# Filler matmuls around the first transposes, one product moved in each expert's last weight chunk, and one set of weight sums issued later: a routed mixture of experts behind linear attention

## The chip, the cores and the metric

The kernel runs on one core of one Trainium2 chip. The metric is the device time of one execution in microseconds (us). Three executions of the kernel before took 555.15 us (median), from 554.48 to 555.25. A core has a matrix engine (PE, with its weight loads shown apart as PEld), a vector engine (DVE), a scalar engine (ACT), a general engine (POOL) and a queue that only issues DMAs (SP). Each engine works through its own list in order; semaphores tie the lists together. PE writes to PSUM only, and ACT and DVE read it from there.

## The reference

```python
kv  = einsum('bhsd,bhse->bhde', k, v)          # 8 batches, 8 heads, s = 576, d = 64, no softmax
out = einsum('bhsd,bhde->bhse', q, kv)
x   = out / sqrt(mean(out*out, -1) + 1e-6) * g_norm      # 4608 tokens of 512 values
e_idx = argmax(x @ w_gate)                     # one of 8 experts for each token
gate  = softmax(x @ w_gate)[e_idx];  eom = sigmoid(x @ w_output_gate)
for e in range(8):                             # each token goes through its expert alone
    h = relu(x[e_idx == e] @ w1[e])            # 512 -> 1024
    y[e_idx == e] = gate * eom[:, e] * (h @ w2[e])       # 1024 -> 512
```

All inputs and outputs are float32.

## The kernel before

**First part: attention and routing.** For each batch PE builds `kv` (`kv_step`), then the 36 row tiles of `out`, 128 tokens each (`out_tile`). ACT squares them, DVE sums the squares (`sums`), and `route` works out experts, weights and row numbers for three groups of tiles (16, 10 and 10) in steps. Rows go to a buffer in device memory (`xs`), from which POOL gathers each expert's tokens by index. `p1_main` sets the order of this part by hand. After the last row tile it works through the string `TAIL`, letter by letter in `act` (L1010): `Q` evacuates the rows left, `W` issues weight loads, a digit takes the next step of that group's routing, `C` calls `constant` and `L` takes the next step of `lead_run`. `constant(ps, n)` (L685) issues n bfloat16 matmuls of ones by ones, 256 columns wide here, whose results nobody reads. `C` issues eight of them into a PSUM tile of the pool `ps_b` (three buffers, tag `big`).

`lead_run` starts the fullest expert before the routing of the last group is known. Its first two steps (`stage`, L280) each take one gathered tile of 128 tokens: DVE scales it by its norms, PE transposes it in four matmuls (L296), ACT copies it out (L299). Its next eight (`lead1`, L317) are the first layer for one eighth of the hidden values each, four full float32 matmuls (L325). Between those steps the string puts routing of group 2, whose rank matmuls (L888 to L895) stand behind the second `lead1`.

**Second part: experts.** `RUNS` has nine runs. Run 0 is the lead, run 1 the rest of the lead expert, runs 2 to 8 are the other seven experts with room for 656, 632, 608, 592, 572, 560 and 544 tokens. Each float32 operand is split into a rounded high part and a residual low part, and each product is three matmuls (high by high, high by low, low by high). From run 2 on the first layer is done by a scheme of seven products instead of eight per pair of blocks: `seven(i)` is a generator that goes through four weight chunks (c = 0 to 3), and `begin(i, n)` takes its next n steps. For one chunk, `a` and `d` are two PSUM tiles (`hpsa`, `hpsd`):

- 11 into `a`, copied by ACT to `sn[0]`; S3 into `d`; 12 into a third tile; S2 added into `a`, copied to `sn[1]`;
- S1 added into `a`, copied by ACT to `sn[2]` (L545); DVE adds `d` and `sn[2]` (L546); then `split_h` makes the hidden values: ACT applies relu (L499), DVE subtracts for the residual (L502);
- `late3`: S4 added into `a`, which must wait for the copy L545; then `split_h` straight from PSUM;
- `late4`: 22 with T4 added into `d`, which must wait for DVE's read of `d` (L546); DVE adds `d` and `sn[1]` (L513) and `split_h` follows on twice the width.

The `late` steps of a chunk are issued within the next chunk: between S2 and S1 of chunk c stand `late3(c - 1)` and `late4(c - 1)`.

The second layer is `mm2(i, k, events)`: tile k of run i, eight f-steps of three matmuls 128x512 (L591), with `events` called after each f-step. The first tile of a run carries the last two steps of `seven`, `late3(3)` behind f = 0 and `late4(3)` behind f = 1. What comes after it for the next run is put in the same way (`put`, L1271): `x_stage(i + 1, k)` behind f = 2 of tile k (PE transposes two gathered tiles, L445, ACT and DVE make the operands, L454 to L464), `x_sums` behind f = 7 (L471, L472), `sums_of(i + 1, c)` behind f = 1 of tile c - 1, `scale_rows` behind f = 3 of the first tile, `w_split` later. `sums_of` is `w_sums` (L382): four POOL instructions (L387 to L390) that form sums and differences of weight blocks. `scale_rows` is one POOL instruction per gathered tile (L270), which is told to start only behind a certain DVE instruction (`latest`): the two behind f = 3 start behind L458 and L461 of the `x_stage` at f = 2.

In this text the seam of a run is the stretch from its last S1 to the end of its first second-layer tile.

## Time and profile before

| | |
|---|---|
| median of three executions | 555.15 us (554.48 to 555.25) |
| the profiled execution | 558.12 us |
| span of its instructions | 556.3 us |
| PE, PEld busy | 536.3 us (96%), 459.4 us (83%) |
| DVE, ACT, POOL busy | 388.7 us (70%), 296.1 us (53%), 264.6 us (48%) |
| mean granted clock of TensorE | 0.992 |

Busy shares are means over stages with different limits. A PE that is 96% busy leaves 20 us of idle time, and a busy PE can be at half of its clock; both are found only by looking at the stretch in question. In the rows of a timeline a bracket at the end gives the idle time of the engine just before the instruction and what ended it.

### The profile page before, as it was taken

The numbers are of one execution on the slowest core, as the hardware profiler recorded it, in microseconds if no ns is written. First come the engines' busy times: TensorE is split into PE (matmuls) and PEld (weight loads), VectorE is DVE, ScalarE is ACT, GpSimd is POOL, SyncE is SP. The second block draws the span as 40 slices with busy tenths as digits, with TensorE's granted clock in tenths as the row PEclk, the third lists the DMA queues.
The fourth block names the chain that finished last, engine by engine and source line by source line (L and its number), as shares of the span: only waits on it lengthen the run. The fifth ranks groups of instructions, "written<-read, shape, count | busy, mean of one in ns | idle before, by whom it ended". The sixth has DMA issues, their size and how long they took to land.

```text
span 556.3 us, 10940 instructions
## 1 busy us (share of the span) xinstructions
PE 536.3 (96%) x4076; PEld 459.4 (83%) x4076; DVE 388.7 (70%) x828; ACT 296.1 (53%) x604; POOL 264.6 (48%) x283
## 2 busy tenths in 40 slices
PE   9999986999999999999999999999999999999995
PEld 7798885856988978898789878987798789789974
DVE  2135998666699789567976896687578977996600
ACT  1577773143467637364646474646473856475410
POOL 3001224054897288208941792289228933981021
PEclk9999999799999999999999999999999999999999
DMA  8999999653406340616052605251534055214000
GB/s 301 418 417 415 416 395 413 254 185 121 131 1 210 111 140 38 209 41 206 20 189 80 199 38 190 92 163 39 189 93 156 38 193 157 78 64 167 1 37 31
DMA packets 28423, 92.27 MB, mean 166 GB/s; under 512 B 3825, under 2 KB 3825, under 8 KB 28368
## 3 DMA queue, kind: packets, MB, share of 16 engines
q1 hardware_dynamic: 21936, 71.63, 35.5%
q0 software_dynamic: 6432, 19.92, 10.7%
q8 instruction: 33, 0.54, 0.4%
q14 instruction: 22, 0.18, 0.1%
HBM read 72.34 MB, written 19.70 MB: 165 GB/s over the span
## 4 chain that ended last, share of the span: by engine, by line
PE 66%; DVE 14%; DMA 6%; POOL 5%; issue 4%; ACT 3%; SPq 1%; POOLq 0%; DVEq 0%; ACTq 0%
PE yps L591 27%; PE hpsa L479 13%; PE hpsd L479 6%; PE hps L479 4%; PE hps L346 3%; PE yps L585 3%; PE hps L325 3%; DVE hT L502 3%; PE ops L781 2%; DVE ss L807 2%; DMA ld<-qT 2%; DMA xg<-xs,gidx 2%; DMA ld<-kvm 2%; PE kvp L706 2%; POOL xg L270 2%
## 5 line engine op out<-in xcount | busy, mean ns | idle before, releaser
L591 PE MATMUL yps<-whi,hT 128*128 128x512 f32 (+3 forms) x560 | 184.9, 396 | 0.4 <-DVE hT L502 0.4
L591 PEld LDWEIGHTS yps<-whi,hT 128*128 128x128 f32 (+3 forms) x560 | 103.8, 186 | 24.2 <-DVE hT L502 1.3
L591 PE MATMUL yps<-wlo,hT 128*128 128x512 f32 (+3 forms) x280 | 110.0, 393 | 0.0
L605 POOL DMA_INDIRECT out<-y,oidx x42 | 52.0, 1237 | 111.7 <-ACT y L604 76.0
L252 POOL DMA_INDIRECT xg<-xs,gidx x42 | 45.0, 1071 | 96.7 <-ACT hT L499 28.2
L502 DVE SCALAR_TENSOR_TENSOR hT<-ct,hT 128x256 fp32r<-128x256 f32 (+6 forms) x88 | 52.2, 623 | 22.7 <-ACT hT L499 21.8
L591 PEld LDWEIGHTS yps<-wlo,hT 128*128 128x128 f32 (+3 forms) x280 | 52.1, 186 | 9.9
L499 ACT ACTIVATE hT<-ct 128x328 fp32r<-128x328 f32 (+13 forms) x56 | 34.4, 615 | 43.0 <-DVE ct L513 43.0
L270 POOL TENSOR_TENSOR xg<-xg 128x512 f32<-128x512 f32 (+8 forms) x40 | 46.5, 1175 | 10.1 <-DVE ct L534 9.5
L479 PE MATMUL hpsd<-xT,wh 128*128 128x328 f32 (+6 forms) x224 | 48.0, 302 | 1.6 <-DVE ct L546 1.6
L479 PE MATMUL hpsa<-xb,wh 128*128 128x328 f32 (+6 forms) x224 | 48.2, 303 | 1.1 <-ACT sn L545 0.6
L479 PE MATMUL hpsa<-xT,wh 128*128 128x328 f32 (+6 forms) x224 | 47.4, 299 | 0.0
L229 DVE TENSOR_TENSOR wlo<-wraw,whi 128x1024 fp32r<-128x1024 f32 x32 | 40.3, 1260 | 6.5 <-ACT whi L226 6.3
L807 DVE TENSOR_REDUCE ss<-sq 128x8 f32<-128x512 f32 x36 | 23.8, 681 | 30.1 <-ACT sq L797 30.1
L404 DVE SCALAR_TENSOR_TENSOR wl<-wraw,gcol,wh 128x512 fp32r<-128x512 f32 (+1 forms) x56 | 42.6, 800 | 0.1
L781 PE MATMUL ops<-aug,ld 64*128 64x80 f32 (+1 forms) x640 | 39.4, 271 | 1.9 <-ACT gp L798 1.5
L479 PEld LDWEIGHTS hpsa<-xb,wh 128*128 128x128 f32 x224 | 36.6, 188 | 4.9 <-ACT sn L545 3.6
L479 PEld LDWEIGHTS hpsd<-xT,wh 128*128 128x128 f32 x224 | 36.6, 188 | 4.7 <-DVE ct L546 3.9
L604 ACT ACTIVATE y<-yps,tl 128x512 f32<-128x512 f32 (+3 forms) x37 | 25.5, 689 | 28.0 <-PE yps L591 18.7
L404 DVE SCALAR_TENSOR_TENSOR wl<-ws,gcol,wh 128x1024 fp32r<-128x1024 f32 x28 | 40.0, 1429 | 0.0
L781 PEld LDWEIGHTS ops<-aug,ld 64*128 64x128 f32 (+1 forms) x640 | 33.9, 176 | 5.3 <-ACT gp L798 1.7
L479 PEld LDWEIGHTS hpsa<-xT,wh 128*128 128x128 f32 x224 | 37.0, 188 | 1.5
(231 smaller groups left out, 1150.4 us busy)
## 6 DMA issues: line engine op xcount, KB each, us to landing
wraw<-w SPq DMA_DIRECT2D x64, 512.0 KB
ld<-kvm SPq DMA_DIRECT2D x32, 512.0 KB
ld<-qT SPq DMA_DIRECT2D x18, 512.0 KB
xs<-xrow SPq DMA_DIRECT2D x9, 528.0 KB
xs<-xrow SPq DMA_DIRECT2D x2, 1320.0 KB
xs<-xrow SPq DMA_DIRECT2D x1, 2112.0 KB
ld<-rem SPq DMA_DIRECT2D x4, 512.0 KB
xg<-xs,gidx POOLq DMA_INDIRECT x42, 5.0
```

The lines of the kernel that those rows point to most:

```text
L229: eng.tensor_tensor(out=lo, in0=r, in1=hi.bitcast(F32), op=ALU.subtract)
L252: gathered = nc.gpsimd.indirect_dma_start(out=x[:M, :], out_offset=None, in_=rows, in_offset=bass.IndirectOffsetOnAxis(ap=gidx[:M, p, t:t ...
L270: return eng.tensor_tensor(out=v, in0=v, in1=f, op=ALU.mult)
L404: nc.vector.scalar_tensor_tensor(out=lo, in0=x, scalar=gcol[:, 0:1], in1=hi.bitcast(F32), op0=ALU.mult, op1=ALU.subtract)
L479: nc.tensor.matmul(ps, W[a][d], X[b][d], start=start and k == 0, stop=k == 5, skip_group_check=not start)
L499: S.activation(hh, x, AF.Relu)
L502: V.scalar_tensor_tensor(out=v(o, j1 - j0), in0=x[..., j0:j1], scalar=0.0, in1=hh[..., j0:j1].bitcast(F32), op0=ALU.max, op1=ALU.subtract)
L591: nc.tensor.matmul(ps[:M], a, b, start=(f == 0 and j == 0), stop=(f == 7 and j == 2))
L604: nc.scalar.activation(y[:M], ps[:M], AF.Copy, scale=tl[:M, 0:1])
L605: i_ = nc.gpsimd.indirect_dma_start(out=out, out_offset=bass.IndirectOffsetOnAxis(ap=oidx[:M, p, t:t + 1], axis=0), in_=y[:M], in_offset=N ...
L781: nc.tensor.matmul(v[r0:r0 + m, u, p, :], qt[g // 2][r, p, q0:q0 + m], augs[b % 3][r, p, :], start=True, stop=True)
L807: nc.vector.tensor_reduce(out=o, in_=sq, axis=AX.X, op=ALU.add)
```

## The change

Three edits. In `TAIL` two more `C` (sixteen matmuls) stand ahead of the lead's first transposes, and a new letter `c` behind each of the two transposes issues six of the same matmuls into a part of `kvp` that is no longer read. In `seven`, for c = 3 alone, `late4(2)` moves from ahead of S1 to behind it. The number of steps of the generator stays 28. The sums of weight chunk 1 for the next expert are issued behind f = 4 of the first tile instead of f = 1, in runs 2 to 7, and so behind `x_stage` (f = 2) and the two `scale_rows` (f = 3).

```diff
-TAIL = "QW112CCCCCCCLL2L2L22L2L1L2L1K2LL"
+TAIL = "QW112CCCCCCCCCLcLc2L2L22L2L1L2L1K2LL"
@@ seven
             if c:
                 late3(c - 1)
                 yield
+            if c in (1, 2):
                 late4(c - 1)
                 yield
             product(a, w_of(c, "S1"), x_of(i, "T1"), False)
...
             split_h(c, 0, 0, ct[:, 2 * n:3 * n])
             yield
+        late4(2)
+        yield
         late3(3)
         yield
         late4(3)
@@ act
+        elif step == "c":
+            constant(kvp[:, 256:512], 6)
@@ body
                 for c in range(1, 4):
-                    put(order[c - 1], 1, sums_of, p + 1, c)
+                    put(order[c - 1], 4 if c == 1 and i > 1 else 1, sums_of, p + 1, c)
```

Of the kernel before, what the change touches and what calls it, by code (L numbers as in the profile page):

```python
# [71 lines left out]
PLACES = ['VP', 'VP', 'V']  # L72

HOOKS = {35: "G"}
TAIL = "QW112CCCCCCCLL2L2L22L2L1L2L1K2LL"

COLD = (24, (8, 8, 10, 5), 5, 4, 12, 8)

# [57 lines left out]
def body(ctx: ExitStack, tc: tile.TileContext, kvm, rem, qT, wg, gn, w1, w2, kc, xs, tab, out):  # L136
# [31 lines left out]
    kvp, mrp = (ps_y.tile([P, 512], F32, name=n, tag=t) for n, t in (("kvp", "y0"), ("mrp", "y1")))  # L168
# [4 lines left out]
    def take(shape, dt, name):  # L173

        i = (rfree if name == "xrow" else free).pop(0)
        t = mem.tile(shape, dt, name=name, tag=f"slot{i}")
        held[id(t)] = (i, t)
        return t

    def give(t):  # L180
        i, t = held.pop(id(t))
        (rfree if loads and i >= SLOTS - ROWS else free).append(i)
# [12 lines left out]
    def wload(p, which, c, eng=None):  # L195
        r = take([P, 1024], F32, "wraw")
        eng = eng or nc.sync
        src = (w1 if which == 1 else w2)[ds(expert(p, eng), 1), c]
        d = eng.dma_start(out=r, in_=src.rearrange("o p x -> p (o x)"))
        raw[(p, which, c)] = r  # L200
        return d
# [106 lines left out]
    def half(i):  # L308

        n = RUNS[i][2] % P  # L310
        return n if n <= P // 2 else 0

    def place(i):

        return -(-half(i) // 32) * 32
# [94 lines left out]
    def w_drop(c):  # L410
        for w in wop.pop(c):
            give(w)

    def w_of(c, name):
        h0, l0, h1, l1 = wop[c]
        k = ("11", "12", "22").index(name) if name[0] != "S" else int(name[1]) - 1
        a, b = (h1, l1) if name[0] == "S" else (h0, l0)
        return [[x[:, 2 * k + d] for d in range(2)] for x in (a, b)]

    def x_of(i, name):  # L420
        bh, bl, th, tl = xop[i]
        k = ("11", "21", "22").index(name) if name[0] != "T" else int(name[1]) - 1
        a, b = (th, tl) if name[0] == "T" else (bh, bl)
        return [[x[:, 2 * k + d] for d in range(2)] for x in (a, b)]
# [50 lines left out]
    def product(ps, W, X, start):  # L475
        k = 0
        for d in range(2):
            for a, b in ((0, 0), (0, 1), (1, 0)):
                nc.tensor.matmul(ps, W[a][d], X[b][d], start=start and k == 0, stop=k == 5,  # L479
                                 skip_group_check=not start)  # L480
                k += 1

    def seven(i):

        nonlocal ny
        p, _, C = RUNS[i]
        n = C // 2
        st = {}
        S, V = nc.scalar, nc.vector

        T, U = half(i), place(i)
        C0 = C - T

        def split_h(c, f, a, x):

            h = hT[i][:, 2 * c + f]
            v = lambda o, k: h[:, o:o + 2 * k].rearrange("q (k a) -> q a k", a=2)[:, a]
            hh = v(0, n)
            S.activation(hh, x, AF.Relu)  # L499
            cut = C0 // 2  # L500
            for o, j0, j1 in ((C0 + 2 * U, 0, cut), (C0 + U, cut, n)) if T else ((C, 0, n),):
                V.scalar_tensor_tensor(out=v(o, j1 - j0), in0=x[..., j0:j1], scalar=0.0,  # L502
                                       in1=hh[..., j0:j1].bitcast(F32), op0=ALU.max, op1=ALU.subtract)

        def late3(c):
            a, d, sn, ct = st[c]
            product(a, w_of(c, "S4"), x_of(i, "22"), False)
            split_h(c, 0, 1, a)

        def late4(c):  # L510
            a, d, sn, ct = st.pop(c)
            product(d, w_of(c, "22"), x_of(i, "T4"), False)
            latest[0] = V.tensor_tensor(out=ct[:, 0:n], in0=d, in1=sn[:, 1], op=ALU.add)  # L513
            split_h(c, 1, slice(0, 2), ct[:, 0:2 * n].rearrange("q (a k) -> q a k", a=2))
            give(st.pop(("sn", c)))
            give(st.pop(("ct", c)))
            w_drop(c)

        for c in range(4):
            a, d = (pools["two"].tile([P, 512], F32, name=f"hps{x}")[:, 0:n] for x in "ad")  # L520
            st["sn", c] = take([P, 1024], F32, "sn")
            st["ct", c] = take([P, 1024], F32, "ct")
            sn = st["sn", c][:, 0:3 * n].rearrange("q (s n) -> q s n", s=3)
            ct = st["ct", c][:, 0:3 * n]
            st[c] = (a, d, sn, ct)
            product(a, w_of(c, "11"), x_of(i, "11"), True)
            S.copy(sn[:, 0], a)
            yield
            product(d, w_of(c, "S3"), x_of(i, "T3"), True)
            yield  # L530
            b = ps_y.tile([P, DM], F32, name="hps2", tag=f"y{ny % 2}")[:, 0:n]
            ny += 1
            product(b, w_of(c, "12"), x_of(i, "21"), True)
            latest[0] = V.tensor_tensor(out=ct[:, 2 * n:3 * n], in0=b, in1=sn[:, 0], op=ALU.add)  # L534
            yield
            product(a, w_of(c, "S2"), x_of(i, "T2"), False)
            S.copy(sn[:, 1], a)
            yield
            if c:
                late3(c - 1)  # L540
                yield
                late4(c - 1)
                yield
            product(a, w_of(c, "S1"), x_of(i, "T1"), False)
            S.copy(sn[:, 2], a)  # L545
            latest[0] = V.tensor_tensor(out=ct[:, n:2 * n], in0=d, in1=sn[:, 2], op=ALU.add)  # L546
            if c == 0:
                hT[i] = hp.tile([P, 8, 2 * C0 + 2 * U], F32R, name="hT")
                if T < U:
                    for o in (C0 + T, C0 + U + T):  # L550
                        V.memset(hT[i].bitcast(F32)[:, :, o:o + U - T], 0.0)
            split_h(c, 0, 0, ct[:, 2 * n:3 * n])
            yield
        late3(3)
        yield
        late4(3)
        xop.pop(i)
        yield
# [126 lines left out]
    def constant(ps, n, start=True):  # L685

        for _ in range(n):
            k = ps.shape[1] // P
            nc.tensor.matmul(ps, ones, ones.unsqueeze(1).to_broadcast([P, k, P]), start=start, stop=start)
# [291 lines left out]
    def advance(gi):  # L981
        if next(routing[gi], 2) == 2:
            del routing[gi]
# [26 lines left out]
    def act(step):  # L1010
        if step.isdigit():
            advance(int(step))
        elif step == "W":
            for c in range(4):
                wload(0, 2, c)
        elif step == "K":
            ranks()
        elif step == "Q":
            while outs:
                out_rows()  # L1020
            while squares:
                sums()
        elif step == "G":
            free.extend(rfree)
            rfree.clear()
            gather(0)
        elif step == "C":
            constant(ps_b.tile([P, 2, 512], F32, name="cps", tag="big")[:, 0, 0:256], COLD[5])
        else:
            next(lead, None)  # L1030

    def p1_main():
# [16 lines left out]
        while done_tiles < NT:  # L1049
            run_out(NT)  # L1050
        for step in TAIL:
            act(step)
# [148 lines left out]
    with tc.manual_schedule(engines=MAN):  # L1201
# [12 lines left out]
        for i in range(len(RUNS)):  # L1214
            p = RUNS[i][0]
# [55 lines left out]
            def put(k, f, e, *a):  # L1271
                at.setdefault(k, {}).setdefault(f, []).append(lambda: e(*a))

            order = list(range(T))
# [11 lines left out]
                        put(order[0], 1, wload, p + 1, 1, c)  # L1286
            if change:
                for c in range(1, 4):
                    put(order[c - 1], 1, sums_of, p + 1, c)
                if i == 1:  # L1290
                    places = [(1, 0, 4), (2, 3, 0), (3, 3, 4)]
                else:
                    places = [(0, 1, 4), (1, 2, 4), (2, 3, 1), (3, 3, 5)]
                for c, k, f in places:
                    put(order[k], f, w_split, p + 1, c)
                for k in range(3):
                    put(order[k], 2, x_stage, i + 1, k)
                    put(order[k], 7, x_sums, i + 1, k)
                for j in range(2):
                    k = 3 + j + (i == 1)  # L1300
                    put(order[0], 3, scale_rows, i + 1, k, k + 1, j)
                put(end, 0, wload, p + 1, 2, 0)
                for c in range(3):
                    put(end, 2 * c + 1, drop, 2, c)
                    put(end, 2 * c + 1, wload, p + 1, 2, c + 1)
                for f, n in ((1, 1), (3, 2), (5, 1), (8, 1)):
                    put(end, f, begin, i + 1, n)
# [116 lines left out]
```

## Rows read from the trace of the kernel before

**Rows 1.** Page part 2: granted PE clock in 40 equal slices of the span.
```profile
PEclk9999999799999999999999999999999999999999
```
**Rows 2.** Timeline of PE, 84 to 112 us: start, duration, instruction, idle before.
```profile
88.09 4.53 PE L689 MATMUL cps<-ones 128*128 128x256 bf16 x40 [0.17 <-PE cps L689]
94.65 0.63 PE L296 MATMUL tps<-ident,xg 128*128 128x128 f32 x4 [2.03 <-DVE tl L292]
96.00 0.63 PE L296 MATMUL tps<-ident,xg 128*128 128x128 f32 x4 [0.73 <-DVE tl L292]
97.41 6.75 PE L325 MATMUL hps<-xT,wraw 128*128 128x256 f32 x16 [0.78 <-ACT xT L299]
...
104.39 7.14 PE L325 MATMUL hps<-xT,wraw 128*128 128x256 f32 x32
```
**Rows 3.** Window of 1 us: PE, PEld, DVE, ACT, POOL busy, clock, DMA, GB/s.
```profile
97.00:98.00 1.00, 0.59 (x2) 0.50 (x3) 1.00 (x2) 0.36 (x1) 0.00 (x0) 0.50 1.04 399
```
**Rows 4.** Timeline of DVE at the routing of group 2.
```profile
104.59 0.24 DVE L911 TENSOR_TENSOR rw<-mrp,ohb 128x80 f32<-128x80 f32 x1 [3.46 <-PE mrp L895]
```
**Rows 5.** Timeline of POOL: the first gather for run 1.
```profile
117.08 1.04 POOL L252 DMA_INDIRECT xg<-xs,gidx  x1 [20.71 <-DVE gidx L1108]
```
**Rows 6.** Waits over the span: who for whom, total us, times, longest.
```profile
PEld hpsd L479 <- DVE ct L546: 3.9, 6, 1.0
PEld hpsa L479 <- ACT sn L545: 3.6, 6, 0.6
...
PEld hpsa L445 <- POOL xg L270: 2.6, 5, 1.5
```
**Rows 7.** Timeline of PEld at the seams of runs 5 and 8.
```profile
367.04 0.30 PEld L479 LDWEIGHTS hpsa<-xb,wh 128*128 128x128 f32 x2 [0.56 <-ACT sn L545]
369.13 0.30 PEld L479 LDWEIGHTS hpsd<-xT,wh 128*128 128x128 f32 x2 [0.74 <-DVE ct L546]
...
523.43 0.30 PEld L479 LDWEIGHTS hpsa<-xb,wh 128*128 128x128 f32 x2 [0.60 <-ACT sn L545]
```
**Rows 8.** Chain of waits: two products in a row in run 4.
```profile
308.49 1.69 PE hpsa L479 x12
```
**Rows 9.** Timeline of DVE at the seams of runs 4, 5 and 7.
```profile
315.26 2.27 DVE L1187 TENSOR_TENSOR sel<-sel,c 128x352 f32<-128x352 f32 x1
...
366.75 1.96 DVE L502 SCALAR_TENSOR_TENSOR hT<-ct,hT 128x592 fp32r<-128x592 f32 x1 [0.80 <-ACT hT L499]
368.63 0.45 DVE L546 TENSOR_TENSOR ct<-hpsd,sn 128x296 f32<-128x296 f32 x1
...
372.78 0.41 DVE L458 TENSOR_TENSOR xt<-xt,tps 128x256 f32<-128x256 f32 x1
...
478.65 1.82 DVE L502 SCALAR_TENSOR_TENSOR hT<-ct,hT 128x512 fp32r<-128x512 f32 x2 [0.77 <-ACT hT L499]
```
**Rows 10.** Timeline of POOL at the seams of runs 4 and 5.
```profile
315.40 1.06 POOL L270 TENSOR_TENSOR xg<-xg 128x512 f32<-128x512 f32 x1
316.40 0.74 POOL L387 TENSOR_TENSOR ws<-wraw 128x256 f32<-128x256 f32 x1
...
367.01 1.05 POOL L270 TENSOR_TENSOR xg<-xg 128x512 f32<-128x512 f32 x1
...
374.00 0.74 POOL L387 TENSOR_TENSOR ws<-wraw 128x256 f32<-128x256 f32 x1
...
377.90 2.04 POOL L270 TENSOR_TENSOR xg<-xg 128x512 f32<-128x512 f32 x2
```
**Rows 11.** Timeline of PE at the seams of runs 2, 5 and 7.
```profile
207.46 0.73 PE L591 MATMUL yps<-whi,hT 128*128 128x512 f32 x2 [0.42 <-DVE hT L502]
...
377.40 0.38 PE L445 MATMUL hpsd<-ident,xg 128*128 128x128 f32 x2
379.00 0.44 PE L445 MATMUL hpsa<-ident,xg 128*128 128x128 f32 x2 [1.21 <-POOL xg L270]
...
482.06 0.61 PE L591 MATMUL yps<-whi,hT 128*128 128x512 f32 x2
```

## The prediction, made before the changed kernel was run

> **What bounds the kernel now.** I read the page first, for its row of the granted clock: one slice of forty stands below full speed, the eighth, 97 to 111 us [rows 1]. Then the timeline of PE around it. The filler matmuls end at 92.62 (88.09 and 4.53). PE then idles 2.03, 0.73 and 0.78 us around two sets of transposes of 0.63 [rows 2]. Behind that the clock stands at 0.50, that is 1.2 of 2.4 GHz [rows 3]. The price is in the same timeline: the first two steps of `lead1`, 16 records, take 6.75 us, the next four, 32 records, 7.14 [rows 2]. So the first two run at half speed, and PE is what everything waits for there: DVE idles 3.46 us until the rank matmuls that stand behind these two steps [rows 4].
>
> From run 1 on PE is close to always busy, so I read who held it, over the span. Three waits stand out, all at the seams. The weight loads of `late4` wait for the DVE add L546 (six times, 3.9 us), those of `late3` for the ACT copy L545 (six times, 3.6), and the transposes of `x_stage` for POOL's scaling (five times, 2.6) [rows 6]. The timelines of run 5 show how they come about. `late3` stands only one f-step behind S1, and its load waits 0.56 us for the copy; `late4` waits 0.74 [rows 7]. Its add L546 starts at 368.63, late because DVE was in the wide residual of `late4(2)` from 366.75 for 1.96 us [rows 9]. On POOL the scaling of two tiles starts at 377.90, behind the weight sums of chunk 1 that began at 374.00 [rows 10], and the transposes that need the first stand still from 377.40 to 379.00 [rows 11].
>
> **The lead.** Sixteen more matmuls at 4.53 / 40 = 0.113 us are 1.81 us and end at 94.43, inside the idle time that ends at 94.65. Six more, 0.68 us, behind the first transposes run from 95.28 to 95.96, ahead of 96.00, and six behind the second from 96.63 to 97.31, ahead of 97.41 [rows 2]. What hides all of them is that PE waits for a gather, DVE and ACT; if those came earlier, the fillers would cost at most their own 0.1 to 0.7 us at each place. They write PSUM that nobody reads, and no DMA or other engine stands behind them. PE then works from 85 to 97.4 us with no gap over about 0.2, and I expect the clock to stay. The two steps at full speed take 2 x 7.14 / 4 = 3.57 us instead of 6.75. A few rank matmuls overlap both figures, so I take 3.05 and keep 2.9 to 3.2.
>
> Is it kept? The rank matmuls come 3.05 earlier, and DVE, which waited 3.46 for them, follows [rows 4]. The gather for run 1 at 117.08 is released by the indices that DVE works out at the end of that chain [rows 5], so it moves as well, and with it the scaling and run 1. I find nothing there that keeps its own time. The other bound is that a later gather or row write takes all of it back: 0 to 3.2.
>
> **S1 ahead of late4(2).** No instruction is added or taken away. S1 of chunk 3 runs one product, 1.69 / 2 = 0.85 us [rows 8], earlier, and `late3(3)` follows the copy L545 by a product and an f-step instead of an f-step alone. That is more than any load waited (0.6 at most), so these waits go. L546 no longer queues behind the wide residual but ahead of it, so the waits of `late4(3)` go too. The copy of S2's result now has one product of cover, 0.85, before S1 instead of two; ACT begins it at once today, and I cost it at nothing, at most 0.2 in each of seven runs. A wait of PEld is more than PE loses; I take off 0.17 each, about half of the 0.30 of a pair of loads (an estimate from rows 7). Runs 5 to 8 have six of the twelve waits, 0.56 the first and 0.60 the last [rows 7], 4.1 us together: 4.1 - 1.0 = 3.1. Runs 2 to 4 have 3.4: 2.4.
>
> What is late next is the last residual of the seam, the wide L502 of `late4(3)`, which f = 7 of the first tile needs. In run 7 it ends at 480.47 (478.65 and 1.82) [rows 9], and f = 7 reads it at 482.06 [rows 11]: 1.6 us to spare, of which the seam's own gain, about 1.1, takes most. Runs 5 and 6 have no less. But the residuals that read SBUF are held by POOL. The one at 366.75 met a scaling from 367.01 to 368.06 and ended 0.65 behind it at 368.71 [rows 9, 10]; so 0.65 is its own work. After the change the narrow residual of S1 is held there, and the wide one of `late4(2)` comes 1.5 to 2 us later, where the next scaling and the first weight sum (L387) stand back to back. Run 4 shows what that does: `sel`, started at 315.26, ends at 317.53, behind both (317.14) [rows 9, 10].
>
> This is a place where the Trainium skill speaks against the change: its page "GPSIMD Engine Reference", section "Specifications", says that GpSimd shares its SBUF interfaces with VectorE and contends with DVE instructions that have two SBUF inputs. The rows agree in kind; by that rule each seam of runs 2 to 7 would hand over a wide residual to a longer hold, which is the second rival below. Without it the seams would give all of 5.5.
>
> For runs 5 to 7, where no overflow list stands between, I count the wide residual ending about 0.6 behind L387, then two short instructions that read PSUM, the relu and the last residual: about when it ends now, since POOL then has nothing left to do but wait. So 3.1 stands for runs 5 to 8. In runs 2 to 4 DVE also has instructions of the overflow list (L1151 to L1187) there, and f = 7 already waits for the residual in run 2 (0.42) [rows 11]. There PE cannot use its 2.4. At worst the wide residual (0.65) and one more hold by a weight sum (0.74) are added, 1.1 each in runs 2 and 4 after what the narrow one saves, and 0.3 in run 3. So these three runs give between -2.4 and +2.4 us. The `sel` row is the nearest, so I take a loss of 0.6.
>
> **Sums of chunk 1 later.** The two scalings at f = 3 now come ahead of four POOL instructions instead of behind them. They wait for L458 and L461 of `x_stage`. In run 5 POOL is free at 374.00 [rows 10], L458 ends at 373.19 [rows 9], so the first scaling ends at about 375.1, and the transposes want it 0.2 behind 377.40, less 1.0 that the seam gains: 376.6. No wait is left in run 5, which is 1.4 of the total. The five waits sum to 2.6 [rows 6], less 0.07 each as in run 5 (1.45 against the 1.38 beyond the usual 0.2 from 377.40 to 379.00): 2.25. In runs 6 and 7 L458 comes close to where PE now wants the tile, so I count 2.0, with 1.4 and 2.25 as ends. Behind the waiting scalings stand the sums of chunk 1, the output of the first tile and the sums of chunks 2 and 3. POOL idles up to 2 us for L458 and works less hindered after, so the sums of chunk 3 come about 1 us later. ACT's last split of the weights takes them just as they end, so it moves too. PE needs that chunk only in the fourth chunk of the next run, more than 15 us on: nothing.
>
> **The sum.** 3.05 + 3.1 + 2.0 - 0.6 = 7.55 us. The profiled execution took 558.12, of which 556.3 is its span; that becomes 550.6. It lies 3 us above the median of the runs, and the cuts are in the work, not in that difference, so the median goes from 555.15 to 547.6.
>
> **Rivals.**
> - *The clock falls all the same.* For it: two of the gaps are only filled around transposes, which keep their place. Against it: from 88.09 on the fillers alone held full clock, and the gaps that preceded the fall are gone. The lead then gives nothing: 547.6 + 3.05 = 550.7.
> - *The hold by POOL eats the seams.* In runs 2 to 7 f = 7 waits for the last residual as long as PE used to wait before it. The scalings and run 8 keep their gain. For it: run 2 already waits there, and run 7 has 0.5 to spare. Lead 3.05, scalings 1.7, run 8 0.4, less 0.6: 4.55, that is 550.6.
> - *The same hold, but longer than the waits it replaces: slower.* If both wide residuals of a seam are held by a run of POOL instructions, 2.2 us as `sel` was, f = 7 comes 1.7 late (2.2 less the 0.5 to spare) in each of six seams: 10.2 against 3.05 + 2.0 + 0.4, so 555.15 + 4.75 = 559.9. It decides from 0.9 us per seam. Against it: POOL has only four sums left after the edit, so it is idle when the last residual comes.
> - *No change.* Clock and seams both fail and the scalings merely wait for L458: within 1.1 us of 555.15.
>
> **How the numbers follow.** Forecast 0.60, with 545.2 to 549.4 as its own range; POOL eats the seams 0.18; the clock falls 0.10; slower 0.07; no change 0.05. About 0.2% (1.1 us) is what a measurement can tell from no change. The range runs from all of runs 2 to 4 gained and more (547.6 - 3.0 = 544.6) to past both rivals near 550.7, 551.4. Faster 0.88, same 0.05, slower 0.07.
>
> **What would show it.** The clock at 1.00 in every microsecond from 92 to 106, and the first two steps of `lead1` in about 3.6 us; the gather for run 1 near 114. No wait of `hpsa` for L545, none of `hpsd` for L546. Transposes of `x_stage` with no wait for L270 over 0.3. Wrong: a clock of 0.50 anywhere behind the transposes; waits of the products L591 for DVE L502 at f = 7 of runs 5 to 7; or the wide residual of `late4(2)` lasting over 2.5 us.

## The result, and the profile after

The changed kernel takes 548.34 us, the median of six executions (548.08 to 550.05). The kernel before took 555.59 in as many beside it (554.48 to 556.62). The ratio is 0.9873, with a 95% interval of 0.9855 to 0.9891: 1.3% faster. The forecast was 547.6, and its range from 544.6 to 551.4 holds the time. The profiled execution took 548.17, its span is 546.4, and its mean granted clock 0.997.

The page of the kernel after, parts 1 and 2 (busy time of each engine, and the granted clock of PE in 40 slices):

```profile
PE 532.6 (97%) x4104; PEld 461.0 (84%) x4104; DVE 389.8 (71%) x828; ACT 295.3 (54%) x604; POOL 268.3 (49%) x283
...
PEclk9999999999999999999999999999999999999998
```

The seven in the eighth slice [rows 1] is gone. PE's busy time went from 536.3 to 532.6, although 28 fillers more are in it. In the kernel after, lines behind the edits are numbered higher: the copy L545 and the add L546 are L546 and L547, the fillers L692, the second-layer products L594.

The timeline of PE around the lead, of the kernel after; it answers to [rows 2]:

```profile
87.41 6.27 PE L692 MATMUL cps<-ones 128*128 128x256 bf16 x56 [0.17 <-ACT gp L801]
94.09 0.63 PE L296 MATMUL tps<-ident,xg 128*128 128x128 f32 x4 [0.41 <-issue]
94.56 0.82 PE L692 MATMUL kvp<-ones 128*128 128x256 bf16 x6
95.44 0.63 PE L296 MATMUL tps<-ident,xg 128*128 128x128 f32 x4
95.91 0.82 PE L692 MATMUL kvp<-ones 128*128 128x256 bf16 x6
96.85 3.72 PE L325 MATMUL hps<-xT,wraw 128*128 128x256 f32 x16
```

The reader is to see that the brackets of 2.03, 0.73 and 0.78 us are gone but for 0.41, and that the sixteen records of the first two steps last 3.72 us where they lasted 6.75. The window behind the transposes stands at a clock of 1.00 (2.4 GHz), where it stood at 0.50 [rows 3] (columns: PE, PEld, DVE, ACT, POOL busy, clock, DMA, GB/s):

```profile
97.00:98.00 1.00, 1.00 (x5) 0.90 (x6) 0.95 (x2) 0.00 (x0) 0.00 (x0) 1.00 1.07 401
```

The list of waits no longer has any of the three of [rows 6]. What has grown is the waiting of the products of f = 7, in runs 2, 6 and 7: it was 1.6 us of PEld in the kernel before (1.3 for L502 and 0.3 for L499) and is 3.8 now (who for whom, total us, times, longest):

```profile
PEld yps L594 <- ACT hT L499: 2.4, 3, 1.1
...
PEld yps L594 <- DVE hT L502: 1.4, 3, 0.6
...
PE yps L594 <- ACT hT L499: 1.1, 2, 0.7
```

The gather for run 1 starts at 113.47 instead of 117.08 [rows 5].

**Where the time went, in the two profiled executions.** I took the start of the same PE instructions (the transposes of `x_stage` in each run, and the last product of the program) in both traces and subtracted. The columns are us gained in each run; a minus is a loss. The first goes from the last `x_stage` of the run before to f = 2 of the first tile, the second from there to f = 2 of the second tile, so that f = 7 of the first lies in it, and the third on to the `x_stage` of the third tile.

| stretch | seam before f = 2 | over f = 7 | scalings and the rest | sum |
|---|---|---|---|---|
| up to run 2 (the lead) | | | | 3.64 |
| run 2 | 0.67 | -0.53 | -0.04 | 0.10 |
| run 3 | 0.44 | 0.00 | 0.40 | 0.84 |
| run 4 | 1.23 | 0.29 | 0.19 | 1.71 |
| run 5 | 0.91 | 0.00 | 1.44 | 2.35 |
| run 6 | 1.00 | -0.63 | 0.26 | 0.63 |
| run 7 | 1.22 | -0.89 | 0.33 | 0.66 |
| run 8 | 0.49 | | | 0.49 |
| all | 5.96 | -1.76 | 2.58 | 10.42 |

Of the lead's 3.64, 0.56 are there at the first transposes already (94.65 and 94.09); the two steps bring 3.03. Of the 10.42, 0.47 are lost behind the last product: the two profiled executions differ by 558.12 - 548.17 = 9.95, and the medians by 7.25. So nearly 3 us, about what the two steps bring, are not in the medians. That is the question which the first experiments take up.

### The profile page after: what moved, and what is told of

Its sections match the earlier page's. It is cut to its first block, busy times and chain, and to the rows that moved or that the text cites. A ratio compares the mean times of both kernels' runs of the same rounds, so it can differ in the third digit from the quotient of the medians.

```text
span 546.4 us, 11005 instructions
## 1 busy us (share of the span) xinstructions
PE 532.6 (97%) x4104; PEld 461.0 (84%) x4104; DVE 389.8 (71%) x828; ACT 295.3 (54%) x604; POOL 268.3 (49%) x283
## 4 chain that ended last, share of the span: by engine, by line
PE 77%; DVE 12%; DMA 4%; ACT 2%; issue 2%; SPq 1%; POOL 0%; POOLq 0%; DVEq 0%; ACTq 0%
PE yps L594 31%; PE hpsa L479 16%; PE hpsd L479 8%; PE hps L479 4%; PE hps L346 3%; PE yps L588 3%; DVE hT L502 3%; PE hps L325 3%; PE ops L784 2%; DMA ld<-kvm 2%; DMA ld<-qT 2%; DVE ss L810 2%; PE kvp L709 2%; PE tps L445 1%; PE cps L692 1%
## 5 line engine op out<-in xcount | busy, mean ns | idle before, releaser
L594 PE MATMUL yps<-whi,hT 128*128 128x512 f32 (+3 forms) x560 | 185.8, 397 | 1.3 <-ACT hT L499 1.1
L594 PEld LDWEIGHTS yps<-whi,hT 128*128 128x128 f32 (+3 forms) x560 | 103.8, 186 | 26.3 <-ACT hT L499 2.4
L594 PE MATMUL yps<-wlo,hT 128*128 128x512 f32 (+3 forms) x280 | 110.1, 393 | 0.0
L608 POOL DMA_INDIRECT out<-y,oidx x42 | 47.3, 1127 | 94.2 <-ACT y L607 57.4
L252 POOL DMA_INDIRECT xg<-xs,gidx x42 | 43.6, 1038 | 94.0 <-ACT hT L499 28.3
L502 DVE SCALAR_TENSOR_TENSOR hT<-ct,hT 128x256 fp32r<-128x256 f32 (+9 forms) x88 | 47.0, 564 | 22.7 <-ACT hT L499 22.7
L594 PEld LDWEIGHTS yps<-wlo,hT 128*128 128x128 f32 (+3 forms) x280 | 52.1, 186 | 9.8
L499 ACT ACTIVATE hT<-ct 128x328 fp32r<-128x328 f32 (+13 forms) x56 | 34.3, 613 | 43.5 <-DVE ct L513 43.5
L270 POOL TENSOR_TENSOR xg<-xg 128x512 f32<-128x512 f32 (+8 forms) x40 | 43.6, 1101 | 17.0 <-DVE ct L534 9.5
L404 DVE SCALAR_TENSOR_TENSOR wl<-wraw,gcol,wh 128x512 fp32r<-128x512 f32 (+1 forms) x56 | 46.1, 861 | 0.2 <-ACT wh L403 0.2
L404 DVE SCALAR_TENSOR_TENSOR wl<-ws,gcol,wh 128x1024 fp32r<-128x1024 f32 x28 | 42.4, 1514 | 0.0
```

Of the source, the lines that this page charges most:

```text
L252: gathered = nc.gpsimd.indirect_dma_start(out=x[:M, :], out_offset=None, in_=rows, in_offset=bass.IndirectOffsetOnAxis(ap=gidx[:M, p, t:t ...
L270: return eng.tensor_tensor(out=v, in0=v, in1=f, op=ALU.mult)
L404: nc.vector.scalar_tensor_tensor(out=lo, in0=x, scalar=gcol[:, 0:1], in1=hi.bitcast(F32), op0=ALU.mult, op1=ALU.subtract)
L499: S.activation(hh, x, AF.Relu)
L502: V.scalar_tensor_tensor(out=v(o, j1 - j0), in0=x[..., j0:j1], scalar=0.0, in1=hh[..., j0:j1].bitcast(F32), op0=ALU.max, op1=ALU.subtract)
L594: nc.tensor.matmul(ps[:M], a, b, start=(f == 0 and j == 0), stop=(f == 7 and j == 2))
```

## The experiments

**One part at a time: the lead alone, the moved product alone, the later sums alone.** These three, and the fourth below, ran beside 22 executions of the kernel before (median 555.36, from 554.27 to 558.38).

```diff
 # e1_lead_only: TAIL and the letter c, nothing else
-TAIL = "QW112CCCCCCCLL2L2L22L2L1L2L1K2LL"
+TAIL = "QW112CCCCCCCCCLcLc2L2L22L2L1L2L1K2LL"
+        elif step == "c":
+            constant(kvp[:, 256:512], 6)
```

> Only the fillers at the lead. Theory (the clock): the clock stays at 1.00 from 92 to 106 us, the first two steps of the lead's first layer take about 3.7 us instead of 6.75, and all of it is kept to the end: 3.1 us, so about 552.4 against 555.5. Rival (given back later): the first gather for run 1 or the weights arrive when they did, and less than 1 us is left: 554.6 or more.

Measured: 555.05 us (554.12 to 555.79, twelve executions), ratio 0.9985, interval 0.9970 to 1.0000. At most 1.7 us and about 0.3 came of the edit, not 3.05. Yet its profile shows the edit at work: the two steps take 3.72 us at full clock, and PE's last product starts at 546.86 instead of 549.88, 3.02 earlier. So the saving is real against that one profile of before and not against its median. The spread says the same: of the twelve executions none is above 555.79, while 15 of 39 executions of the kernel before (22 here, 17 in the second group) are; the means differ by 0.8 (555.80 and 555.02). The mean granted clock goes the same way, though it is no sure mark (the profiled execution of before has 0.992): 12 of the 39 have 0.991 or less and a median of 556.78, the other 27 have 555.10, and none of the twelve of this kernel has a clock below 0.993.

```diff
 # e2_late4_only: in seven, for c = 3
+            if c in (1, 2):
                 late4(c - 1)
...
+        late4(2)
+        yield
         late3(3)
```

> Only the move of S1 ahead of late4(2). Theory (the two seam edits need each other): the waits for L545 and L546 go, 5.5 us of them, but the scaling of the fourth tile still stands behind the sums of chunk 1, whose time POOL sets, so in runs 3 to 7 the transposes of the second x_stage wait longer by what the seam gained; runs 2 and 8 keep theirs: 1 to 1.5 us, about 554.3, with waits of hpsa for L270 of about 6 us in place of 2.6. Rival (the edits add up): about 4.5 us, 551.0, and the waits for L270 stay at 2.6.

Measured: 559.12 us (555.83 to 563.11, ten executions), ratio 1.0057, interval 1.0028 to 1.0086. Alone the moved product makes the kernel slower, which neither theory had. The waits of its profiled execution, which was the fastest of the ten:

```profile
PEld hpsa L445 <- POOL xg L270: 5.9, 5, 2.6
...
PE hpsa L445 <- POOL xg L270: 4.7, 3, 2.4
```

The waits for L545 and L546 are gone, as after the whole change, but the one for POOL's scaling has grown from 2.6 to 5.9. The timeline of POOL in run 4 of this kernel says why:

```profile
312.24 1.06 POOL L270 TENSOR_TENSOR xg<-xg 128x512 f32<-128x512 f32 x1
313.24 0.75 POOL L387 TENSOR_TENSOR ws<-wraw 128x256 f32<-128x256 f32 x1
...
316.75 0.73 POOL L387 TENSOR_TENSOR ws<-wraw 128x256 f32<-128x256 f32 x1
...
318.25 1.70 POOL L389 TENSOR_TENSOR ws<-wraw 128x256 f32<-128x256 f32 x1
319.91 0.72 POOL L390 TENSOR_TENSOR ws<-wraw,ws 128x256 f32<-128x256 f32 x1
320.59 2.04 POOL L270 TENSOR_TENSOR xg<-xg 128x512 f32<-128x512 f32 x2
```

From 312.24 to 322.6 POOL has no gap over 0.1: the sums of chunk 0 and those of chunk 1 stand in a row ahead of the last two scalings. PE reaches the transposes sooner and waits 2.41 us for them. By the subtraction of the table, against the kernel before, runs 2 to 8 gain 6.0 us at the seams, lose 2.7 over f = 7 and lose 3.3 at the scalings: nothing is left of the gain, of which this queue takes one part and the residuals that f = 7 waits for the other. Why other executions of it are up to 7 us longer still, the last experiment asks.

```diff
 # e3_sums_only
-                    put(order[c - 1], 1, sums_of, p + 1, c)
+                    put(order[c - 1], 4 if c == 1 and i > 1 else 1, sums_of, p + 1, c)
```

> Only the sums of chunk 1 issued later. Both theories: the five waits of the transposes for L270 go, 2.1 us, about 553.4; the waits for L545 and L546 stay as they were. If the scaling only changes its wait to L458, nothing is gained: 555.5.

Measured: 552.25 us (551.99 to 554.29, seven executions), ratio 0.9945, interval 0.9921 to 0.9969. The wait for L270 is gone from its list, and those for L545 and L546 stand as before (4.2 us in seven and 3.7 in six). So 3.1 us come of this edit alone, 1.0 more than was expected. By the subtraction of the table 2.6 are at the scalings, and 0.3 each in runs 2 and 4 over f = 7: in the kernel before the last residual of those seams stood beside the sums of chunk 1, and here it does not. That residual in run 2 (two instructions in one row), in the kernel before and then here:

```profile
206.28 1.75 DVE L502 SCALAR_TENSOR_TENSOR hT<-ct,hT 128x640 fp32r<-128x640 f32 x2 [0.87 <-ACT hT L499]
```

```profile
202.96 0.91 DVE L502 SCALAR_TENSOR_TENSOR hT<-ct,hT 128x640 fp32r<-128x640 f32 x2 [0.86 <-ACT hT L499]
```

The lead of this kernel has the old fillers, and still:

```profile
97.18 3.72 PE L325 MATMUL hps<-xT,wraw 128*128 128x256 f32 x16 [0.78 <-ACT xT L299]
```

The brackets around the transposes are 1.46, 0.73 and 0.78 us (2.03, 0.73 and 0.78 in the kernel before), and the two steps run at full clock. The windows of the same trace show where its half clock is instead, twelve microseconds earlier, in the fillers:

```profile
85.00:86.00 1.00, 0.60 (x4) 0.40 (x4) 1.00 (x3) 1.00 (x4) 0.00 (x0) 0.50 1.05 412
97.00:98.00 1.00, 0.82 (x4) 0.74 (x5) 1.00 (x2) 0.13 (x1) 0.00 (x0) 1.00 1.03 393
```

There it costs nothing, since what the fillers take comes out of PE's wait for the gathered tile. So the theory that the gaps around the transposes always bring the fall is refuted by this trace.

**Does the lead of the kernel before always fall?** Two kernels ask this: the kernel before once more, and the kernel with none of the fillers ahead of the lead, which gives the price of a fall that is certain. The second group ran beside 17 executions of before (median 555.50, from 554.12 to 558.45).

The first is the kernel before without any edit.

> The kernel before, unchanged, profiled a second time. Theory (the place of the fall varies): the profiled execution of before was one of its slow ones, because the clock happened to fall on the lead; this one takes about 555.3, the first two steps of the lead's first layer take 3.7 us and the half clock lies elsewhere, most likely within the fillers between 84 and 89 us. Rival (the fall is always there): 6.75 us again, and 558.

Measured: 558.03 us in one profiled execution, which again has the fall on the lead:

```profile
97.98 5.78 PE L325 MATMUL hps<-xT,wraw 128*128 128x256 f32 x16 [0.78 <-ACT xT L299]
```

That was not expected of this execution; but its time, 2.5 us above the median, is that of the first profile. Over all traces here whose lead has the old fillers, the two steps ran at half clock in two (the kernel before, twice) and at full clock in four (e2, e3, and e6 and e8 below). The two at half clock took 558.12 and 558.03. Over the three traces with the new fillers (the changed kernel, e1, e4) it is none.

```diff
 # e7_no_fillers
-TAIL = "QW112CCCCCCCLL2L2L22L2L1L2L1K2LL"
+TAIL = "QW112LL2L2L22L2L1L2L1K2LL"
```

> The kernel before without any filler ahead of the lead's transposes (seven fewer C), so that PE is idle for some 9 us there and the clock is low in every execution when the lead begins. This measures the price of the fall: 3 to 4 us, 558.5 to 559.5, if a fall on the lead is kept to the end; 555.5 if it is given back.

Measured: 557.91 us (556.59 to 559.37, ten executions), ratio 1.0037, interval 1.0018 to 1.0056. The clock stands at half from 83 to 104 us, and the rows of its lead are:

```profile
95.06 1.09 PE L296 MATMUL tps<-ident,xg 128*128 128x128 f32 x4 [8.36 <-DVE tl L292]
...
98.28 6.57 PE L325 MATMUL hps<-xT,wraw 128*128 128x256 f32 x16 [0.78 <-ACT xT L299]
```

So a certain fall on the lead costs 557.91 - 555.50 = 2.4 us against a kernel in which it falls in some executions, 2.8 against the 555.10 of those with the higher clock, and it is kept to the end: the price in the prediction was about right, its frequency was not.

**The two seam edits without the fillers.** This is the changed kernel with the old `TAIL`.

```diff
 # e6_both_seam_edits, against the changed kernel
-TAIL = "QW112CCCCCCCCCLcLc2L2L22L2L1L2L1K2LL"
+TAIL = "QW112CCCCCCCLL2L2L22L2L1L2L1K2LL"
```

> The move of S1 and the later sums together, without the fillers. If the fillers are worth about 0.8 us (what they gave alone), 549.0, some executions 2 to 3 us above that; if they are worth 3.1 in every execution, 551.4.

Measured: 549.38 us (547.91 to 552.05, six executions), ratio 0.9897, interval 0.9869 to 0.9924. The two seam edits together give 6.1 us, where the sums alone gave 3.1 and the product alone lost 3.8. The fillers are worth about 1.0 on top of them (549.38 against 548.34, in different groups of runs; their intervals overlap), 0.3 on top of the kernel before. Its profiled execution has the full clock on the lead (3.72) and takes 547.91, no more than the changed kernel's 548.17.

**What the seams still hand back.** In runs 2, 6 and 7 the changed kernel loses 0.5 to 0.9 us over f = 7. The rival that POOL eats the seams names the wide residual. Runs 2, 6 and 7 are also those of runs 2 to 7 whose last tile has at most 64 tokens (16, 60 and 48); there `split_h` makes every residual in two instructions, in runs 3 to 5 in one. The timeline of DVE in run 6 of the changed kernel (the second part of the narrow residual of S1, both parts of the wide one, and the last residual with its parts in one row), then that of POOL:

```profile
412.70 1.50 DVE L502 SCALAR_TENSOR_TENSOR hT<-ct,hT 128x30 fp32r<-128x30 f32 x1
...
415.35 2.15 DVE L502 SCALAR_TENSOR_TENSOR hT<-ct,hT 128x512 fp32r<-128x512 f32 x1 [0.79 <-ACT hT L499]
...
417.42 0.75 DVE L502 SCALAR_TENSOR_TENSOR hT<-ct,hT 128x60 fp32r<-128x60 f32 x1
...
419.75 0.82 DVE L502 SCALAR_TENSOR_TENSOR hT<-ct,hT 128x512 fp32r<-128x512 f32 x2 [0.78 <-ACT hT L499]
```

```profile
413.08 1.05 POOL L270 TENSOR_TENSOR xg<-xg 128x512 f32<-128x512 f32 x1
...
415.20 1.07 POOL L270 TENSOR_TENSOR xg<-xg 128x512 f32<-128x512 f32 x1
416.20 0.74 POOL L387 TENSOR_TENSOR ws<-wraw 128x256 f32<-128x256 f32 x1
417.02 1.07 POOL L388 TENSOR_TENSOR ws<-ws,wraw 128x256 f32<-128x256 f32 x1
```

Two instructions of the same forms, 512 and 60 columns, take 0.82 us together with POOL idle (the row at 419.75) and 2.82 beside it, from 415.35 to 418.17. The first part ends 0.56 behind L387 (416.94), about as forecast; the second, 0.21 where POOL is idle, lasts until just behind the third POOL instruction (418.09). Ahead of them 30 columns of the narrow residual lasted 1.50, until just behind a scaling (414.13). In run 5, where each residual is one instruction, the narrow one ends at 360.52, ahead of the scaling at 360.80, and the wide one keeps its 0.81, ahead of the next:

```profile
361.70 0.81 DVE L502 SCALAR_TENSOR_TENSOR hT<-ct,hT 128x592 fp32r<-128x592 f32 x1 [0.80 <-ACT hT L499]
...
363.34 1.06 POOL L270 TENSOR_TENSOR xg<-xg 128x512 f32<-128x512 f32 x1
```

That the two parts are why these runs are the ones that lose is read from the rows; no run here makes them one instruction. That POOL's sums hold the wide residual can be tested. If that is the cause, the sums of chunk 0 held until the seam is over must end it. The next kernel takes them out of the end of `seven` and puts them behind f = 1 of the first tile, to start only behind the add L513 of `late4(3)`; the rest is the changed kernel.

```diff
 # e4_sums0_held, against the changed kernel
-                    if c == 3 and change:
-                        sums_of(p + 1, 0)
...
+                if i > 1:
+                    put(order[0], 1, w_sums, p + 1, 0, 0)
...
     def w_sums(p, c, after=None):
+        first = g.tensor_tensor(out=S[:, 0], ...)
+        if after is not None:
+            behind(first, latest[after])
```

> The changed kernel, and the sums of chunk 0 as well are held: their first instruction waits for the add L513 of late4(3), so that no weight sum stands right behind the last scaling while the wide residual of late4(2) waits. Theory (POOL's run of two instructions holds that residual, and so f = 7 waits in runs 2, 6 and 7): the residual of 2.3 to 2.8 us there falls by about 0.7, the waits of f = 7 for L499 and L502 fall from 3.8 us of PEld to under 1.5, and the kernel is 0.8 to 1.6 us faster than the changed one, about 547.1. Rival (DVE's queue is simply too long there): the waits stay, and later sums make it the same or slower, 548.3 to 549.5.

Measured: 545.60 us (544.47 to 547.95, six executions), ratio to the kernel before 0.9818, interval 0.9791 to 0.9845. It beats both kernels; against the changed one it is 2.7 us less, in another group of runs, where 0.8 to 1.6 were expected. In this kernel L499, L502 and L513 are L501, L504 and L515. Its timelines in run 6, DVE and then POOL:

```profile
413.77 1.61 DVE L504 SCALAR_TENSOR_TENSOR hT<-ct,hT 128x512 fp32r<-128x512 f32 x2 [0.79 <-ACT hT L501]
...
416.95 1.37 DVE L504 SCALAR_TENSOR_TENSOR hT<-ct,hT 128x512 fp32r<-128x512 f32 x2 [0.79 <-ACT hT L501]
```

```profile
413.62 1.06 POOL L270 TENSOR_TENSOR xg<-xg 128x512 f32<-128x512 f32 x1
416.30 0.74 POOL L387 TENSOR_TENSOR ws<-wraw 128x256 f32<-128x256 f32 x1 [1.62 <-issue]
```

The wide residual now meets the scaling alone and ends 0.7 behind it (415.38, 414.68). The last residual is the one beside the sums now (1.37 where it took 0.82), and f = 7 comes late enough for that: no wait of the products for the relu or the residual is left in the list of waits. By the same subtraction as in the table, e4 gains on the changed kernel 1.4 us in run 2, 0.7 in run 6 and 0.9 in run 7, 3.0 together, and nothing over 0.1 in any other run.

Runs 2 and 6 show the cause; run 7 does not. There the scalings of e4 also come later against PE (the first waits 1.89 us for its gather to land), and the trace of e6, with the seams of the changed kernel and the sums of chunk 0 in their old place, loses nothing in run 7 either (0.01 over f = 7, against 0.53 and 0.64 lost in runs 2 and 6). Its first scaling there waits 1.35 us for its gather, and the wide residual lasts 1.38:

```profile
464.98 1.38 DVE L502 SCALAR_TENSOR_TENSOR hT<-ct,hT 128x512 fp32r<-128x512 f32 x2 [0.79 <-ACT hT L499]
```

So 2.1 of the 3.0 us are shown to come of the held sums, and whether run 7 hands anything back differs between executions.

**Why the moved product alone varies so much.** The kernel e2 once more, unchanged, for another profile.

> The move of S1 alone, unchanged, profiled a second time: its ten executions lay between 555.8 and 563.1, with mean clocks from 0.995 down to 0.982. Theory: behind waits of about 2 us for the scaling (runs 4 and 5) the clock falls in some executions; if this one is above 557, its rows show a clock of 0.50 behind one of these waits. Rival: another engine is late there at full clock.

Measured: 559.04 us in one profiled execution. Runs 4 and 5 have the waits of 2.4 and 2.0 us again, and run 7 one that the first trace did not have. The timeline of PE there, and the window behind it:

```profile
482.82 0.44 PE L445 MATMUL hpsa<-ident,xg 128*128 128x128 f32 x2 [2.94 <-POOL xg L270]
```

```profile
486.00:487.00 1.00, 1.00 (x4) 0.80 (x3) 1.00 (x3) 1.00 (x2) 1.00 (x2) 0.50 0.17 66
```

Behind the wait the clock stands at 0.50 (1.2 GHz) from 484 to 487.3 (the window from 487 has 0.85), so that this wait costs its 2.9 us and about 1.6 more, half of that stretch. In return f = 7 of that run does not wait, 1.3 us, so that run 7 is 3.3 longer than in the first trace; no other run differs by over 0.1 between the two (559.04 and 555.83). POOL is later there: its first scaling for the next run starts 0.8 later than in e2, and the last two, behind all eight sums, 1.7 later (481.73 and 480.00). In runs 4 and 5 of the same execution no fall followed. That is one part of the spread; that other executions, down to a mean clock of 0.982 at 563.11 us, have more such falls is likely and was not traced.

## Why the prediction was right, point by point

That the time came within 0.8 us of the forecast is luck: two errors of over 2 us cancelled. By the sums below, either alone would have left it inside the range, at about 550.3 or 545.3.

**The lead: the step that failed.** The prediction carries 3.05 us from the profile of before to the median with the sentence that "the cuts are in the work, not in that difference". It was the other way round. The profiled execution lay 3 us above the median because the clock had fallen on its lead, and the lead's 3.05 was the price of that same fall. The mechanism and its size hold: 6.75 us became 3.72, and a fall that always comes costs 2.4. But only two of six traces with the old fillers have it on the lead; in the others it comes in the fillers and costs nothing. In the medians the edit is worth 0.3 to 1.0. What it does is to remove the long executions. Why the clock falls on the lead in some executions and in the fillers in others stays open.

**The seams of runs 5 to 8.** Predicted 3.1. The table has 3.62 ahead of f = 2 (0.91, 1.00, 1.22, 0.49) and 1.52 handed back in runs 6 and 7: 2.1. All waits for L545 and L546 went, as forecast, and over all runs the seams gained 5.96 ahead of f = 2, where the prediction had 5.5 before any loss. The step that the wide residual ends "about 0.6 behind L387" was too short in runs 6 and 7: it counted one instruction where there are two. The first part ended there, the second was held through L388 as well, and both together took 2.82 and 2.83 us. That is past the bound of 2.5 that the prediction named as a sign against itself, and the waits of f = 7 in these two runs are another of its signs.

The Trainium skill, page "GPSIMD Engine Reference", section "Specifications", says that GpSimd contends with VectorE instructions that read two operands from SBUF. The rows of run 6 agree, and give the size that the page leaves out: 0.82, 1.61 and 2.82 us for the same two instructions beside none, one and three of POOL's.

**Runs 2 to 4.** Predicted a loss of 0.6 with bounds of 2.4 on both sides; they gained 2.34 at the seams (0.67, 0.44, 1.23) and lost 0.24 net behind (-0.53, 0, 0.29, the last of which the later sums give alone as well, by e3): 2.1. I took the loss from the `sel` row, a DVE instruction held by POOL [rows 9, 10]. In run 4 of the changed kernel that hold is gone:

```profile
309.00 1.00 DVE L502 SCALAR_TENSOR_TENSOR hT<-ct,hT 128x608 fp32r<-128x608 f32 x1 [0.83 <-ACT hT L499]
309.92 0.51 DVE L1192 TENSOR_TENSOR sel<-sel,c 128x352 f32<-128x352 f32 x1
```

The whole seam moved 1.2 us earlier against POOL's list, where scalings and gathers follow each other at their own pace, so the wide residual and `sel` (2.27 before, 0.51 now) ended ahead of the third scaling (310.82). I had moved DVE's instructions among themselves and left POOL's where they were. By these rows, whether a run gains or loses goes by where the residual falls against L270, L387 and L388; run 2 lost in the way that was feared, run 4 did not.

**The scalings.** Predicted 2.0, measured 2.58 with the rest of their column, 1.37 of it in run 5, where 1.4 was forecast. That the next POOL instructions come later harmed nothing: no wait of PE for them is in the list. What the prediction did not see is that the two seam edits need each other: the moved product gains only once the sums are out of the way (6.1 together, 3.1 and -3.8 alone).

**The sum.** From 555.4, the median of the 39 executions of before: 6.8 for the seams and scalings (5.96 - 1.76 + 2.58, from two profiled executions) and 0.3 for the lead (from medians) make 548.3, which is what was measured; the medians of e6 split the same total as 6.1 and 1.0, and the runs do not decide between the two. The prediction had 2.7 too much for the lead and 2.3 too little for the rest, and began 0.2 lower, at 555.15. Of its rivals, that POOL eats the seams holds in part in three of six runs of the profiled execution, and e4 shows it for two of them (2.1 us); the one that is slower describes no run of it, since no seam has both wide residuals held: the last one lasts 1.35 at most.

## What to carry to other kernels

Before a cost is taken from one profiled execution, compare that execution's time with the median: where it is longer by about the cost that you want to remove, that cost may be what made it longer, and the median does not have it. Two edits on one seam are to be costed together, since a wait that goes hands its time to whoever is late next: here the scaling behind eight POOL instructions, then the residual behind three. A row that merges two instructions (x2) is to be taken apart before it is costed, since a short second part can be held as long as a long one. An instruction of VectorE that reads both operands from SBUF should not be timed from a row where POOL was idle if the edit moves it to where POOL is busy.

## What the runs showed of the hardware that was not expected

- With the same instructions and the same gaps, the place of the half clock differs between executions: on the lead in the two traces at 558.1 and 558.0 us, in the fillers at 84 to 89 us in others. It is in both places in the trace of e5, of which this is the window ahead of its first steps:

```profile
96.00:97.00 1.00, 0.89 (x4) 0.71 (x4) 1.00 (x4) 0.68 (x1) 0.48 (x1) 0.50 1.03 407
```

- A residual of 0.82 us (two instructions) lasted 2.82 beside three POOL instructions in a row, while the next one, which reads PSUM (L502 from `hpsa` at 418.10, beside L389), kept its 0.51. Its first part got through between the second and the third: it ended at 417.50, while L388, begun at 417.02, lasted 1.07 where L387 and L389 around it took 0.74. Its second part, of 60 columns, ended only behind L388.
- In run 2 two instructions of eight columns with a single input were held too: L1157 and L1158, 0.69 and 0.65 us beside L388 and L389 of POOL, and the same two (L1159 and L1160 in e4) took 0.17 each where POOL was idle.

```profile
199.69 0.69 DVE L1157 CAST cei<-cnp 128x8 int32<-128x8 f32 x1
200.42 0.65 DVE L1158 TENSOR_SCALAR cei<-cei 128x8 int32<-128x8 int32 x1
```
